# Low bits of weight words kept in PSUM, eight short warm-up series and a new order table in a local-attention and gated-convolution kernel

## The chip, the cores and the metric

One core of a Trainium2 chip runs the whole kernel. TensorE (PE) multiplies matrices and writes its sums to PSUM; VectorE (DVE), ScalarE (ACT) and GpSimd (POOL) do the elementwise work; SyncE (SP) starts the transfers in the order of its queue. The metric is device time per execution in microseconds, the median of the runs.

## The reference

There are 4 batches of 768 positions with 8 heads of 64 (512 columns). The first stage is attention: every query sees the keys less than 16 positions away and, beside them, 24 pooled keys, each the largest entry by column of a block of 32 keys; the pooled values are block means.

```
scores_l = scale * q @ k.T, where |i - j| < 16, else -1e9
scores_s = scale * q @ k_max + log(32)        # k_max: 24 blocks
a = softmax(concat(scores_l, scores_s)); x = a @ concat(v, v_mean)
```

The second stage takes x as (batch, position, 512). A causal convolution of five taps by column gives a gate, and two 512x512 matrices frame it:

```
gate = 1 / (1 + exp(-conv5(x, conv_w)))
out = (gate * (x @ w_val)) @ w_out
```

q and k are drawn at 0.8, conv_w at 24 / sqrt(5), x and the result are float32. The two matrices and conv_w reach the kernel as float64 words.

## The kernel before

A tile of queries has 64 positions; a group g is four of them (256 positions, all 512 columns), and there are 12 groups, three to a batch. A unit u is half a group: two head pairs, so that unit u belongs to group u // 2 and there are 24.

For one unit the work goes through these steps, each named by a letter in the order table: `S` score products on TensorE (two per unit, by head pair), `N` mask and row minimum on VectorE (four), `E` exponentials with row sums on ScalarE (four steps of two activations and two reads of the accumulator), `R` reciprocals, `M` the scaling by them on GpSimd (two), `T` transposes on TensorE, `C` their eviction on ScalarE (two), `X` the product with the values. `F` and `H` copy its result to SBUF (float32 and rounded to the matrix format), `L` is the rest that the rounding lost, `I`, `A` and `G` are the convolution (a first tap, four more taps of two column blocks on VectorE, a tanh), all by unit. For a group there are `V` (product with w_val, two per group), `gf`, `gh`, `gl` (gating, rounding and rest), `O` (product with w_out, two per group), `oe` (eviction of the output) and `st` (its store).

The first batch has a special way to its pooled values: `VB` sums them on TensorE into the two tiles `vb`, and `X` of group 0 multiplies with them apart. For the other groups small copies `f` write the pooled rows into the value tile (four per group, waiting for that tile's loads). Group 0 also does its `V` and `O` in float32, in one series of four terms each, from the tile `wf`; all others use the split weights (high and low part, `wvc`/`wvb`, `woc`/`wob`).

The matrices come as float64 words in four blocks of 128 rows. A block's path is: load (`w.k`, `o.k`), `rescale` on ScalarE (line 387, `wvs`, `wos`: the high word as a float, rebiased), `low_bits` on VectorE (line 395, `wvd`, `wod`: the low word shifted right by 29), `join` on VectorE (line 402, `wve`, `woe`: high part shifted and or-ed with the low bits). `cs`, `cd`, `ce` do the same for the 20 convolution weights. Both matrices go through the one tile `wf`, one behind the other: the second can be written only after group 0's `V` has read the first.

The order of all work is a table written out by hand, `ORDER` (line 53): the program walks over its tokens and issues each, so every engine, and SP's queue too, works through its own share in that order and waits where something isn't ready. `psum_plan` (line 131) gives each PSUM tile one of four single banks (`p`) or two double ones (`s`, for scores and transposes) by the first and the last token that uses it; a tile that takes a bank waits until the one before it has been read. `pw` (line 329) are products of a constant tile with itself, whose result nobody reads: six series of two, all in one bank that they hold from the first to the last of them.

Of the kernel before, what the change touches and what calls it, by code (L numbers as in the profile page):

```python
# [53 lines left out]
k.0.1 mset pw.0 q0.1 ks.0.1 k.0.0 ks.0.0 kc.0.1 S.0.1 pw.1 pw.2 kc.0.0 c cs q0.0 m N.0.3 E.0.3 N.0.2
E.0.2 S.0.0 N.0.1 E.0.1 N.0.0 E.0.0 q.1 S.2.0 N.2.1 S.2.1 k.0.3 ks.0.3 q0.3 n.0.2 VB.2 kc.0.3 pw.3
E.2.1 S.1.1 N.2.0 E.2.0 N.2.2 E.2.2 N.2.3 E.2.3 S.3.1 k.0.2 q0.2 ks.0.2 N.1.3 E.1.3 R.0 kc.0.2 n.0.4
w.0 wvs.0 i h.0 S.1.0 N.1.1 E.1.1 cd ce N.1.2 E.1.2 S.3.0 N.3.1 N.1.0 n.0.0 pw.4 VB.4 wvd.0 E.1.0
w.1 wvs.1 N.3.2 wve.0 N.3.3 VB.0 n.0.5 wvd.1 M.0.1 M.0.0 T.0 C.0.1 C.0.0 R.1 M.1.1 n.0.3 VB.5 VB.3
N.3.0 R.2 E.3.1 E.3.0 q.2 S.5.1 S.5.0 E.3.3 wve.1 E.3.2 N.5.0 M.2.1 N.5.3 N.5.2 N.5.1 S.4.1 wvc.1
S.4.0 n.0.1 VB.1 M.1.0 T.1 vb.0 vb.1 C.1.0 E.5.0 R.3 N.4.3 v.0.1 v.0.0 w.3 wvs.3 X.0 I.0.1 F.0 I.0.0  # L60
N.4.1 wvd.3 N.4.0 N.4.2 wve.3 w.2 wvd.2 C.1.1 M.3.0 wvc.0.1 v.1.1 X.1 v.1.0 A.0.0 A.0.1 A.0.2 M.3.1
A.0.3 k.1.3 wvb.0 M.2.0 T.2 wvs.2 E.5.1 wve.2 I.1.1 F.1 A.0.4 I.1.0 A.1.0 A.0.5 wvb.1 k.1.0 h.1
wvc.2.1 A.1.1 A.0.6 ks.1.3 kc.1.3 T.3 C.3.0 V.0.0 C.2.1 E.5.2 C.2.0 wvc.3.1 A.0.7 k.1.1 ks.1.1
kc.1.1 ks.1.0 wvb.3 kc.1.0 E.5.3 R.5 E.4.3 M.5.1 q.3 S.6.1 E.4.2 n.1.1 E.4.0 A.1.2 M.5.0 pw.5 G.0
N.6.3 gf.0.0 A.1.3 E.4.1 N.6.2 A.1.4 R.4 f.1.0.1 f.1.1.0 f.1.1.1 f.1.0.0 X.2 C.3.1 H.2 k.1.2 M.4.0
X.3 F.2 F.3 I.2.0 H.3 ks.1.2 I.3.0 S.6.0 N.6.0 N.6.1 v.2.1 T.5 C.5.1 C.5.0 A.1.5 v.2.0 A.3.0 A.2.0
I.3.1 S.7.1 A.1.6 A.3.1 A.1.7 A.3.2 kc.1.2 S.7.0 N.7.0 A.3.3 o.1 E.6.0 E.6.2 n.1.0 q.4 N.7.3 A.3.4
N.7.2 A.3.5 M.4.1 T.4 E.6.3 C.4.0 G.1 C.4.1 I.2.1 E.7.3 E.7.0 N.7.1 A.3.6 V.0.1 wod.1 tr.1.1 S.9.0
tr.1.0 gf.0.1 o.0 A.3.7 A.2.1 wod.0 A.2.2 wos.0 wos.1 woe.0 woe.1 G.3 f.2.0.0 f.2.0.1 o.2 E.7.2
S.8.1 wvb.2 L.3 wod.2 S.8.0 S.9.1 f.2.1.0 f.2.1.1 o.3 X.5 wod.3 wos.2 woe.2 h.2 L.2 woc.1.1 wos.3  # L70
woe.3 n.1.3 tr.1.3.1 F.5 E.6.1 H.5 E.7.1 X.4 F.4 H.4 woc.2 O.0.1 oe.0.1 O.0.0 A.2.3 R.6 M.6.0 A.2.4
N.9.0 M.6.1 A.2.5 N.8.3 A.2.6 R.7 A.2.7 I.5.0 G.2 I.5.1 I.4.0 N.8.1 N.8.0 N.9.1 n.1.2 tr.1.2 N.8.2
A.4.0 woc.0 v.3.0 k.2.2 k.2.3 N.9.2 A.4.1 A.5.0 v.4.1 E.8.0 n.2.0 oe.0.0 q.5 A.4.2 A.5.1 v.3.1 E.8.2
V.1.1 N.9.3 VS.1 A.5.2 gf.1.1 E.8.3 I.4.1 vs.1 T.6 L.4 M.7.0 M.7.1 T.7 C.6.1 wob.0 E.9.1 v.4.0 C.7.1
ks.2.3 kc.2.3 A.5.3 k.2.1 A.4.3 C.7.0 L.5 woc.3.1 wob.3 gh.1.1 A.5.4 f.3.1.0 f.3.0.0 f.3.0.1 wob.2
A.5.5 h.3 C.6.0 E.8.1 E.9.2 V.1.0 A.4.4 A.4.5 f.3.1.1 f.4.0.0 S.11.1 S.11.0 A.5.6 ks.2.2 kc.2.2
S.10.0 A.5.7 E.9.0 G.5 A.4.6 S.10.1 gf.1.0 R.8 M.8.0 A.4.7 k.3.2 X.7 wob.1 gl.1.1 M.8.1 X.6 E.9.3
V.2.1 N.10.1 N.11.0 G.4 N.11.2 N.10.3 N.11.3 N.10.0 N.10.2 H.7 F.7 gh.1.0 I.7.0 R.9 I.7.1 q.6 k.2.0
st.0.0 v.5.0 A.7.0 E.10.0 M.9.0 M.9.1 gf.2.1 V.2.0 q.7 f.4.1.1 f.4.0.1 f.4.1.0 T.9 E.10.3 A.7.1
I.6.0 F.6 A.7.2 gl.1.0 E.10.2 H.6 ks.2.1 I.6.1 N.11.1 E.10.1 A.7.3 st.0.1 k.3.0 v.5.1 ks.2.0 kc.2.1  # L80
A.6.0 A.7.4 A.7.5 T.8 A.6.1 C.8.0 R.10 C.9.1 E.11.3 C.9.0 C.8.1 A.6.2 A.7.6 E.11.0 A.6.3 gf.2.0 h.4
L.7 kc.2.0 tr.2.0 O.1.0 oe.1.0 A.6.4 S.13.0 S.12.1 S.12.0 S.13.1 A.7.7 N.13.1 A.6.5 M.10.1 L.6
M.10.0 E.11.1 E.11.2 A.6.6 R.11 M.11.0 M.11.1 G.7 X.8 n.2.1 tr.2.1 f.5.1.0 gh.2.0 gl.2.0 H.8 X.9 F.9
O.1.1 A.6.7 N.12.3 G.6 N.13.0 st.1.0 N.12.1 f.5.0.0 N.13.3 N.12.2 q.8 n.2.2 I.8.1 I.8.0 F.8 I.9.0
oe.1.1 N.13.2 N.12.0 h.5 A.8.0 A.8.1 I.9.1 E.12.3 H.9 L.9 T.10 C.10.1 gh.2.1 T.11 C.11.1 E.12.1
E.12.2 C.10.0 A.9.0 C.11.0 gl.2.1 L.8 A.9.1 A.9.2 A.9.3 A.9.4 V.3.0 A.8.2 tr.2.2 gf.3.0 v.6.0 v.6.1
A.9.5 E.13.2 E.12.0 A.9.6 A.9.7 k.3.3 A.8.3 A.8.4 A.8.5 A.8.6 A.8.7 R.12 M.12.0 O.2.0 G.9 E.13.1
oe.2.0 V.3.1 gf.3.1 E.13.3 E.13.0 M.12.1 gh.3.1 n.2.3 tr.2.3 f.5.0.1 f.5.1.1 X.11 I.11.1 X.10 G.8
gl.3.1 I.11.0 H.11 S.14.1 S.15.0 n.3.1 st.2.0 R.13 S.14.0 F.11 S.15.1 VS.2 vs.2 k.3.1 O.2.1 F.10
I.10.1 H.10 I.10.0 N.15.1 N.14.0 A.11.0 N.15.0 N.15.2 N.14.1 A.11.1 A.11.2 N.15.3 A.11.3 M.13.0  # L90
N.14.3 V.4.0 A.10.0 N.14.2 A.10.1 A.10.2 A.10.3 oe.2.1 E.15.0 L.10 h.6 gf.4.0 M.13.1 n.3.2 tr.3.2
st.1.1 gh.3.0 gl.3.0 T.13 E.14.0 T.12 C.12.1 E.14.1 V.4.1 gh.4.0 gl.4.0 E.14.3 C.13.1 E.14.2 C.12.0
A.11.4 A.10.4 A.11.5 ks.3.1 A.11.6 A.11.7 O.3.0 ks.3.0 kc.3.0 S.17.1 C.13.0 E.15.1 L.11 f.6.0.1
E.15.2 gf.4.1 tr.3.1 S.17.0 G.11 f.6.0.0 v.7.0 f.6.1.1 A.10.5 A.10.6 A.10.7 ks.3.3 R.14 M.14.1
M.14.0 S.16.0 st.2.1 E.15.3 G.10 gh.4.1 v.7.1 S.16.1 N.16.2 N.16.1 n.3.3 oe.3.0 q.9 f.6.1.0 X.13
H.13 F.13 X.12 F.12 I.13.1 I.13.0 kc.3.1 R.15 M.15.0 N.16.0 N.17.3 N.16.3 N.17.0 ks.3.2 N.17.1
N.17.2 E.17.3 E.17.2 V.5.0 I.12.0 H.12 E.17.0 T.14 M.15.1 n.3.0 tr.3.0 gf.5.0 C.14.0 f.7.0.1 A.12.0
f.7.0.0 I.12.1 E.16.0 tr.3.3 gl.4.1 A.13.0 A.13.1 kc.3.3 A.13.2 A.13.3 A.12.1 T.15 A.13.4 A.12.2
A.12.3 E.17.1 R.17 A.12.4 A.13.5 A.13.6 C.14.1 A.12.5 O.3.1 C.15.0 gh.5.0 oe.3.1 E.16.2 V.5.1 gf.5.1
M.17.1 L.12 E.16.3 q.10 O.4.0 v.8.0 f.7.1.0 st.3.1 f.7.1.1 E.16.1 R.16 M.16.1 oe.4.0 C.15.1 v.8.1  # L100
X.14 gl.5.0 kc.3.2 h.7 X.15 A.13.7 G.13 A.12.6 A.12.7 F.15 I.14.0 G.12 S.18.1 S.18.0 S.19.0 st.4.0
f.8.1.1 S.19.1 q.11 gh.5.1 gl.5.1 O.5.0 N.18.1 H.14 F.14 M.17.0 L.14 I.14.1 I.15.1 H.15 L.15 M.16.0
I.15.0 oe.5.0 N.18.3 N.18.0 N.19.1 N.19.0 A.14.0 E.19.0 st.3.0 f.8.1.0 f.8.0.0 f.8.0.1 N.19.3 N.19.2
A.14.1 A.14.2 N.18.2 E.19.2 L.13 O.4.1 oe.4.1 VS.3 h.8 T.16 C.16.1 A.14.3 A.14.4 A.14.5 A.14.6
A.15.0 A.14.7 C.16.0 E.18.3 G.14 v.9.0 v.9.1 vs.3 f.9.0.0 st.5.0 T.17 C.17.0 C.17.1 A.15.1 A.15.2
E.18.2 V.6.1 gf.6.1 A.15.3 A.15.4 A.15.5 A.15.6 V.6.0 gf.6.0 f.9.1.0 E.18.1 E.18.0 R.18 E.19.1
E.19.3 R.19 X.17 F.17 H.17 M.19.1 X.16 I.16.0 v.11.1 f.9.1.1 A.15.7 G.15 H.16 F.16 gh.6.1 I.16.1
S.23.1 gl.6.1 S.20.1 S.20.0 S.23.0 N.23.0 M.19.0 N.20.2 N.20.1 E.20.1 E.20.2 A.16.0 N.20.3 N.23.3
N.23.1 A.16.1 V.7.1 O.5.1 gh.6.0 E.20.3 N.23.2 A.16.2 gf.7.1 N.20.0 I.17.1 I.17.0 oe.5.1 M.18.1
M.18.0 T.18 C.18.1 gh.7.1 gl.6.0 h.9 T.19 C.19.1 st.4.1 O.6.1 V.7.0 A.17.0 A.17.1 A.17.2 st.5.1  # L110
v.11.0 f.9.0.1 C.19.0 C.18.0 A.17.3 A.17.4 A.17.5 A.16.3 f.11.1.0 f.11.0.0 E.23.3 E.23.1 E.20.0
oe.6.1 A.16.4 A.16.5 A.17.6 A.16.6 A.16.7 A.17.7 gf.7.0 X.19 R.20 L.17 M.20.1 X.18 E.23.2 G.16
S.22.0 S.21.0 S.22.1 S.21.1 L.16 V.8.1 G.17 E.23.0 R.23 M.23.0 I.18.1 I.18.0 N.21.1 gh.7.0 H.19
gl.7.0 gl.7.1 F.18 v.10.0 F.19 H.18 L.19 N.21.2 E.21.2 N.21.3 O.7.1 st.6.1 v.10.1 f.11.1.1 N.21.0
E.21.0 f.10.1.1 f.10.0.0 A.18.0 A.18.1 N.22.0 A.18.2 gf.8.1 I.19.0 I.19.1 A.18.3 M.20.0 E.21.1
E.21.3 R.21 oe.7.1 V.8.0 M.21.1 st.7.1 A.19.0 A.19.1 f.10.0.1 A.19.2 A.19.3 N.22.1 A.19.4 O.6.0
M.21.0 T.21 gf.8.0 gh.8.0 M.23.1 N.22.2 E.22.2 E.22.1 L.18 N.22.3 A.19.5 A.18.4 oe.6.0 st.6.0 A.18.5
T.20 C.20.1 O.7.0 A.19.6 A.19.7 E.22.3 E.22.0 R.22 C.21.1 gh.8.1 gl.8.0 V.9.1 C.20.0 A.18.6 G.19
gl.8.1 f.10.1.0 M.22.1 M.22.0 h.10 oe.7.0 st.7.0 gf.9.1 C.21.0 A.18.7 G.18 X.20 f.11.0.1 X.21 F.20
I.20.1 H.20 I.20.0 T.23 A.20.0 T.22 O.8.0 I.21.0 I.21.1 H.21 F.21 C.22.0 A.20.1 A.20.2 A.21.0 A.21.1  # L120
A.21.2 A.21.3 A.21.4 A.20.3 A.21.5 L.21 oe.8.0 st.8.0 gh.9.1 A.20.4 A.20.5 A.20.6 O.8.1 oe.8.1
st.8.1 C.22.1 C.23.0 C.23.1 V.9.0 L.20 V.10.0 h.11 gl.9.1 A.21.6 A.21.7 gf.9.0 gh.9.0 gl.9.0 A.20.7
G.20 X.23 F.23 H.23 L.23 G.21 X.22 I.23.0 gf.10.0 gh.10.0 I.23.1 O.9.1 oe.9.1 O.9.0 H.22 I.22.0 F.22
# [582 lines left out]
```

## Time and profile before

| | before |
|---|---|
| median of 3 runs | 240.81 us (240.70 to 241.55) |
| profiled execution | 242.98 us, span 241.2 us |
| TensorE busy | 221.4 us (92%), 2884 records |
| ScalarE | 186.4 us (77%) |
| VectorE | 171.4 us (71%) |
| GpSimd | 155.8 us (65%) |
| transfers | 46.42 MB, mean 192 GB/s |
| mean granted TensorE clock | 0.991 |

The span runs from the first to the last instruction of the core; the time of an execution is a little longer. The profiled execution is one of its own and took longer than the median of the runs. The busy shares are means over the span, and the stretches of the kernel differ: the rows further down are read by stretch.

### The profile page before, as it was taken

Reading aid. Unit: us, or ns where it says so; the run is one execution under the profiler, and the core shown is the slowest. Engines: PE = TensorE matmul, PEld = TensorE weight load, DVE = VectorE, ACT = ScalarE, POOL = GpSimd, SP = SyncE. Lnnn points to the kernel's source line nnn. Section 1 sums busy time; section 2 is a strip of 40 time slices with the busy share of each in tenths; the row PEclk is TensorE's granted clock in tenths of the full one; section 3 lists DMA queues with packets and bytes.
Section 4 is the critical chain, followed back from the end, with each engine's and each line's share of the span. In section 5 each row is a group of like instructions: output and inputs, shape, how many; then the busy total and the mean of one; then the engine's idle time right before and its main releaser. Section 6 shows DMA issues by size and latency. Waiting matters only on the chain.

```text
span 241.2 us, 7772 instructions
## 1 busy us (share of the span) xinstructions
PE 221.4 (92%) x2884; PEld 187.3 (78%) x2884; DVE 171.4 (71%) x683; ACT 186.4 (77%) x614; POOL 155.8 (65%) x219
## 2 busy tenths in 40 slices
...
DMA packets 17318, 46.42 MB, mean 192 GB/s; under 512 B 2400, under 2 KB 3424, under 8 KB 17280
## 3 DMA queue, kind: packets, MB, share of 16 engines
...
q8 instruction: 23, 0.38, 0.6%
q14 instruction: 15, 0.12, 0.2%
...
## 4 chain that ended last, share of the span: by engine, by line
PE 71%; POOL 9%; DVE 6%; DMA 5%; ACT 4%; issue 3%; SPq 1%; POOLq 0%; ACTq 0%; DVEq 0%
PE val L567 26%; PE out L596 23%; PE x L513 9%; PE s L444 7%; POOL p L487 4%; PE pt L496 4%; DMA v<-vb 2%; DVE sn L460 2%; POOL vT L326 2%; DMA k<-in_kT_dram 1%; DVE wf L409 1%; POOL xl L533 1%; POOL gl L581 1%; DVE g L547 1%; ACT g L542 1%
## 5 line engine op out<-in xcount | busy, mean ns | idle before, releaser
L547 DVE SCALAR_TENSOR_TENSOR g<-xf,cwt,g 128x256 f32<-128x256 f32 x192 | 88.4, 483 | 12.4 <-ACT g L542 8.8
L474 ACT ACTIVATE p<-sn,nm 128x120 f32<-128x120 f32 x192 | 73.9, 397 | 5.9 <-DVE nm L460 3.0
L487 POOL TENSOR_TENSOR p<-p,ri 128x480 f32<-128x480 f32 x48 | 47.3, 1001 | 22.5 <-DVE ri L482 18.3
L460 DVE CUSTOM_DVE_ANT_0 sn<-s,mask 128x120 f32<-128x120 f32 x192 | 42.4, 276 | 14.7 <-PE s L444 14.3
L567 PE MATMUL val<-xh,wv 128*128 128x256 f32 x352 | 50.1, 284 | 0.0
L567 PEld LDWEIGHTS val<-xh,wv 128*128 128x128 f32 x352 | 45.3, 188 | 1.9 <-issue 0.6
L596 PE MATMUL out<-wo,gh 128*128 128x512 f32 x176 | 45.6, 401 | 0.0
L581 POOL TENSOR_TENSOR gl<-gf,gh 128x512 fp32r<-128x512 f32 x22 | 28.4, 1294 | 19.8 <-ACT gh L576 18.7
L474 ACT ACTIVATION_READ_ACCUMULATOR p<-sn,nm 128x1 f32 x192 | 38.5, 201 | 0.0
L596 PEld LDWEIGHTS out<-wo,gh 128*128 128x128 f32 x176 | 31.8, 188 | 7.4 <-ACT g L542 0.4
L533 POOL TENSOR_TENSOR xl<-xf,xh 128x512 fp32r<-128x512 f32 x22 | 28.4, 1295 | 9.2 <-ACT xf L528 6.6
L444 PE MATMUL s<-k,qbd 64*64 64x120 f32 x768 | 25.3, 279 | 6.8 <-POOL k L315 3.5
L444 PEld LDWEIGHTS s<-k,qbd 64*64 64x64 f32 x768 | 21.1, 140 | 11.0 <-POOL k L315 6.3
L326 POOL TENSOR_TENSOR vT<-vT 128x384 f32<-128x384 f32 (+3 forms) x48 | 27.2, 566 | 2.8
L513 PE MATMUL x<-pts,v 120*64 120x64 f32 x768 | 27.2, 224 | 1.9 <-DMA v<-vb 1.2
L513 PEld LDWEIGHTS x<-pts,v 120*64 120x64 f32 x768 | 25.3, 138 | 3.9 <-issue 1.8
L567 PE MATMUL val<-xl,wv 128*128 128x256 f32 x176 | 27.8, 279 | 0.0
L500 ACT COPY pts<-pt 120x512 f32<-120x512 f32 x48 | 26.7, 592 | 1.4 <-PE pt L496 1.3
L572 DVE SCALAR_TENSOR_TENSOR gf<-gt,val 128x512 f32<-128x512 f32 x24 | 16.4, 685 | 13.2 <-PE val L567 12.8
L596 PE MATMUL out<-wo,gl 128*128 128x512 f32 x88 | 24.3, 396 | 0.2 <-POOL gl L581 0.2
L567 PEld LDWEIGHTS val<-xl,wv 128*128 128x128 f32 x176 | 23.8, 188 | 0.0
L606 ACT ACTIVATE ob<-out 128x512 f32<-128x512 f32 x23 | 13.8, 599 | 11.6 <-PE out L596 7.6
...
## 6 DMA issues: line engine op xcount, KB each, us to landing
v<-in_vw_dram SPq DMA_DIRECT2D x24, 512.0 KB
k<-in_kT_dram SPq DMA_DIRECT2D x16, 478.0 KB
out_dram<-ob SPq DMA_DIRECT2D x23, 256.0 KB
qbd<-in_qT_dram SPq DMA_DIRECT2D x11, 512.0 KB
vT<-in_vT_dram SPq DMA_DIRECT2D x12, 384.0 KB
raw_wv<-in_wv_dram SPq DMA_DIRECT2D x4, 512.0 KB
raw_wo<-in_wo_dram SPq DMA_DIRECT2D x4, 512.0 KB
...
```

What stands on the lines that cost most here:

```text
L326: nc.gpsimd.tensor_tensor(dst, src[:, :, :n], src[:, :, n : 2 * n], ALU.add)
L444: nc.tensor.matmul(sp[64 * e : 64 * e + 64, h, c * KW : c * KW + KW], qbd[g % NQB][64 * h : 64 * h + 64, pr, i * QT : i * QT + QT], ktile( ...
L460: nc.vector.tensor_tensor_reduce(sn[:, n, :], tiles["s", u][:, h, c * KW : c * KW + KW], mask[:, mv, :], -1.0 / math.sqrt(D), 3.0e38, ALU.add,
L474: nc.scalar.activation(p[:, n, :], tiles["sn", u][:, n, :], AF.Exp, bias=tiles["nm", u][:, n : n + 1], scale=-1.0, accum_out=rs[:, u % NRS ...
L487: nc.gpsimd.tensor_tensor(p[:, w], p[:, w], ri[:, w].unsqueeze(2).broadcast_to([P, TPU, KW]), ALU.mult)
L500: nc.scalar.copy(pts[:, :, QT * e : QT * e + QT], tiles["pt", u][:KW, e])
L513: nc.tensor.matmul(dst, v[:KW, i, c0 : c0 + D], src, start=True, stop=g > 0)
L533: nc.gpsimd.tensor_tensor(xl[:, prs(u), :], xf(g)[:, prs(u), HALO:], tiles["xh", g][:, prs(u), :].bitcast(F32), ALU.subtract,)
L547: nc.vector.scalar_tensor_tensor(gt, xf(u // NHP)[:, pr, o : o + SG], cwt[:, pr, o : o + 1], gt, ALU.mult, ALU.add)
L567: nc.tensor.matmul(val[:, r], w, x, start=(n == 0), stop=(n == len(terms) - 1))
L581: nc.gpsimd.tensor_tensor(gl[:, cos, :], tiles["gf", g, cp], tiles["gh", g][:, cos, :].bitcast(F32), ALU.subtract)
L596: nc.tensor.matmul(po, x, w, start=(n == 0), stop=(n == len(terms) - 1))
```

## The change

The shift `low_bits` writes its result to a PSUM tile of its own, and `join` reads it from there and no longer from the target tile. `psum_plan` learns these nine tiles, each of which holds a single bank from shift to join. Every `pw` series gets a bank of its own for as long as it lasts, and there are eight series, one of eight products and seven of two. The order table is replaced as a whole; all other tokens are the same ones as before. The first 17 and the last 5 lines of the new table are shown.

```diff
-NWARM = 2
+NWARM = (8, 2, 2, 2, 2, 2, 2, 2)
...
+mset k.0.0 pw.2 k.0.1 h.0 ks.0.1 kc.0.1 pw.6 pw.0 pw.3 q0.1 S.0.1 q0.0 c k.0.2 ks.0.0 kc.0.0 m S.0.0
+N.0.1 ks.0.2 kc.0.2 cs E.0.1 N.0.0 n.0.2 E.0.0 pw.5 pw.4 VB.2 N.0.2 E.0.2 k.0.3 N.0.3 ks.0.3 q0.2
+S.1.0 N.1.0 N.1.1 E.0.3 E.1.0 q.1 S.3.0 kc.0.3 S.3.1 N.3.0 q0.3 S.1.1 N.1.3 N.1.2 pw.1 N.3.3 N.3.2
+R.0 M.0.0 M.0.1 pw.7 N.3.1 w.1 wvs.1 wvd.1 E.1.1 E.1.2 E.1.3 R.1 M.1.1 w.0 wvs.0 n.0.0 VB.0 wve.1
+E.3.0 n.0.1 S.2.0 S.2.1 N.2.2 N.2.0 cd N.2.3 wvd.0 n.0.5 VB.1 wve.0 N.2.1 n.0.4 i w.2 wvd.2 M.1.0
+E.3.1 wvs.2 E.3.2 ce E.3.3 R.3 T.0 C.0.0 E.2.1 C.0.1 wve.2 wvc.0.1 M.3.1 M.3.0 q.2 n.0.3 VB.4 VB.5
+VB.3 vb.0 w.3 wvd.3 wvs.3 v.0.0 vb.1 S.5.1 S.5.0 N.5.0 wvc.2.1 wve.3 N.5.2 T.1 C.1.0 E.2.2 C.1.1
+N.5.3 N.5.1 v.0.1 X.0 F.0 wvb.2 I.0.0 E.5.1 X.1 I.1.0 F.1 I.1.1 k.1.3 ks.1.3 wvb.0 E.2.3 k.1.2 A.0.0
+ks.1.2 A.0.1 A.0.2 A.1.0 A.1.1 wvc.3.1 A.0.3 A.1.2 S.4.1 T.3 E.2.0 R.2 n.1.1 tr.1.1 kc.1.3 A.1.3
+S.4.0 N.4.0 wvc.1 V.0.1 kc.1.2 I.0.1 A.0.4 A.1.4 A.0.5 A.1.5 E.5.2 A.0.6 v.1.1 v.1.0 E.5.3 k.1.1 o.2
+n.1.3 A.1.6 C.3.1 f.1.0.0 q.3 C.3.0 N.4.2 E.5.0 N.4.3 R.5 N.4.1 h.1 M.2.1 A.1.7 M.2.0 A.0.7 f.1.0.1
+V.0.0 ks.1.1 T.2 E.4.0 wos.2 wvb.1 G.1 G.0 E.4.3 wod.2 gf.0.0 n.1.2 E.4.1 C.2.1 M.5.1 wvb.3 o.0
+wod.0 woe.2 S.7.1 S.7.0 f.1.1.0 f.1.1.1 X.3 k.1.0 ks.1.0 C.2.0 wos.0 X.2 woe.0 o.1 wod.1 gf.0.1 H.3
+F.3 wos.1 woe.1 tr.1.2 kc.1.1 S.6.1 kc.1.0 S.6.0 N.6.1 woc.0 o.3 E.4.2 wos.3 wod.3 woe.3 O.0.0 H.2
+F.2 O.0.1 I.2.1 I.2.0 tr.1.3.1 M.5.0 woc.1.1 N.6.2 N.7.2 I.3.0 E.6.1 I.3.1 N.6.3 A.2.0 A.2.1 N.6.0
+E.6.0 E.6.3 A.2.2 N.7.0 A.2.3 v.3.1 N.7.3 N.7.1 q.4 L.3 n.1.0 v.2.0 v.2.1 tr.1.0 L.2 woc.3.1 A.2.4
+A.2.5 R.4 M.4.0 E.6.2 oe.0.0 oe.0.1 k.2.2 T.5 C.5.0 S.8.1 S.8.0 f.2.0.0 M.4.1 R.6 M.6.1 E.7.2 C.5.1
...
+gf.10.0 gl.9.0 G.21 X.22 I.22.0 H.22 gh.10.0 F.22 L.22 gf.10.1 gh.10.1 X.23 gl.10.0 I.22.1 H.23
+gl.10.1 O.9.0 O.10.1 F.23 oe.9.0 A.22.0 A.22.1 A.22.2 A.22.3 A.22.4 A.22.5 I.23.1 A.22.6 I.23.0
+A.23.0 A.22.7 G.22 A.23.1 A.23.2 A.23.3 A.23.4 A.23.5 L.23 V.11.0 A.23.6 gf.11.0 V.11.1 O.10.0
+oe.10.1 st.10.1 gh.11.0 A.23.7 G.23 oe.10.0 gf.11.1 gh.11.1 gl.11.1 O.9.1 st.9.0 oe.9.1 st.9.1
+st.10.0 gl.11.0 O.11.0 oe.11.0 st.11.0 O.11.1 oe.11.1 st.11.1
...
@@ -147,9 +147,13 @@
             return [("val", a[0], a[1])]
         if name in ("O", "oe"):
             return [("out", a[0], a[1])]
+        if name in ("cd", "ce"):
+            return [("low", "cw", 0)]
+        if name in ("wvd", "wve", "wod", "woe"):
+            return [("low", name[:2], a[0])]
         if name == "VB":
             return [("vb", 0), ("vb", 1)]
-        return {"vb": [("vb", a[0])], "VS": [("vsp", a[0])], "vs": [("vsp", a[0])], "pw": [("pw", 0)]}.get(
+        return {"vb": [("vb", a[0])], "VS": [("vsp", a[0])], "vs": [("vsp", a[0])], "pw": [("pw", a[0])]}.get(
             name, []
         )
 
@@ -328,9 +332,9 @@
 
     def op_pw(k):
         t = tiles["ones"]
-        for j in range(NWARM):
+        for j in range(NWARM[k]):
             nc.tensor.matmul(
-                ps(("pw", 0), [P, DM])[:QT, : QT + BASE], t[:, :QT], t[:, : QT + BASE],
+                ps(("pw", k), [P, DM])[:QT, : QT + BASE], t[:, :QT], t[:, : QT + BASE],
                 start=True, stop=True,
             )
 
@@ -397,17 +401,18 @@
             return
         dst, raw, n, bufs = parts(nm, k)
         low = raw.rearrange("p (n two) -> p two n", two=2)[:, 0]
-        nc.vector.tensor_scalar(dst.bitcast(U32), low, 29, None, ALU.logical_shift_right)
+        t = ps(("low", nm, k), [P, n])
+        nc.vector.tensor_scalar(t.bitcast(U32), low, 29, None, ALU.logical_shift_right)
 
     def join(nm, k):
         if not wide:
             if nm != "cw":
                 nc.vector.tensor_copy(wf[:, k], rawt(nm, k).bitcast(F32))
             return
-        d = parts(nm, k)[0].bitcast(U32)
-        sc = tiles["sc", f"{nm}{k}"]
+        sc, low = tiles["sc", f"{nm}{k}"], tiles["low", nm, k]
         nc.vector.scalar_tensor_tensor(
-            d, sc.bitcast(U32), 3, d, ALU.logical_shift_left, ALU.bitwise_or
+            parts(nm, k)[0].bitcast(U32), sc.bitcast(U32), 3, low.bitcast(U32),
+            ALU.logical_shift_left, ALU.bitwise_or,
         )
 
     def high_part(nm, k, alt=0):
```

## Rows read from the trace of the kernel before

**Rows 1.** Stretches: us, PE, PEld, DVE, ACT, POOL busy, granted clock, DMA share, GB/s.

```profile
0.00:26.43 26.43, 19.40 (x269) 12.20 (x269) 17.17 (x105) 17.60 (x73) 8.26 (x25) 1.00 0.88 314
26.43:57.58 31.15, 24.78 (x489) 21.01 (x485) 26.37 (x90) 26.65 (x90) 23.76 (x37) 0.95 0.97 348
47.05:53.80 6.75, 5.87 (x32) 4.57 (x32) 4.05 (x23) 5.99 (x22) 4.87 (x7) 0.75 0.94 312
57.58:64.70 7.12, 7.12 (x22) 3.29 (x19) 6.94 (x39) 7.12 (x21) 6.81 (x9) 1.00 0.46 151
64.70:237.20 172.50, 170.10 (x2117) 150.80 (x2115) 120.91 (x455) 134.46 (x432) 117.00 (x151) 1.00 0.46 149
237.20:241.20 4.00, 0.00 (x0) 0.00 (x0) 0.00 (x0) 0.60 (x1) 0.00 (x0) 0.88 0.27 106
```

**Rows 2.** TensorE's timeline: start us, us, line, operation, count, idle before and releaser.

```profile
1.51 0.95 PE L332 MATMUL pw<-ones 128*64 128x104 f32 x4 [1.51 <-POOL ones L255]
5.92 1.08 PE L444 MATMUL s<-k,qbd 64*64 64x120 f32 x16 [3.46 <-POOL k L315]
26.43 0.34 PE L513 MATMUL x<-pts,v 120*64 120x64 f32 x4
31.66 1.15 PE L496 MATMUL pt<-ident,p 64*120 64x64 f32 x32
33.19 3.72 PE L567 MATMUL val<-xf,wf 128*128 128x256 f32 x16 [0.38 <-ACT g L542]
53.76 1.87 PE L444 MATMUL s<-k,qbd 64*64 64x120 f32 x64
55.56 2.08 PE L513 MATMUL x<-pts,v 120*64 120x64 f32 x64
57.58 7.13 PE L596 MATMUL out<-wf,gf 128*128 128x512 f32 x16
```

**Rows 3.** Transfers by line: count, KB of each.

```profile
v<-in_vw_dram SPq DMA_DIRECT2D x24, 512.0 KB
k<-in_kT_dram SPq DMA_DIRECT2D x16, 478.0 KB
qbd<-in_qT_dram SPq DMA_DIRECT2D x11, 512.0 KB
vT<-in_vT_dram SPq DMA_DIRECT2D x12, 384.0 KB
raw_wo<-in_wo_dram SPq DMA_DIRECT2D x4, 512.0 KB
vn<-in_vn_dram SPq DMA_DIRECT2D x6, 256.0 KB
```

**Rows 4.** ScalarE's timeline, its first exponential and four steps later on.

```profile
8.14 0.40 ACT L474 ACTIVATE p<-sn,nm 128x120 f32<-128x120 f32 x1 [0.93 <-DVE nm L460]
...
22.01 0.40 ACT L474 ACTIVATE p<-sn,nm 128x120 f32<-128x120 f32 x1
...
25.05 0.62 ACT L417 CAST wv<-wf 128x512 fp32r<-128x512 f32 x1
```

**Rows 5.** Tiles of VectorE: count, ns least/median/most, first and last start.

```profile
L400 DVE TENSOR_SCALAR wf<-raw_wv x4: 415/474/1414, 19.8 to 29.3; 128x512 uint32<-128x512 uint32 x4
L409 DVE SCALAR_TENSOR_TENSOR wf<-sc_wv,wf x4: 679/780/1083, 20.6 to 32.6; 128x512 uint32<-128x512 uint32 x4
...
L572 DVE SCALAR_TENSOR_TENSOR gf<-gt,val x24: 676/686/689, 39.6 to 227.0; 128x512 f32<-128x512 f32 x24
```

**Rows 6.** GpSimd's timeline around the slowest shift.

```profile
28.73 1.72 POOL L421 TENSOR_TENSOR wv<-wf,wv 128x512 fp32r<-128x512 f32 x1
```

**Rows 7.** Waits of SP's queue: in total, times, longest.

```profile
SPq L373 <- DMA v<-in_vw_dram: 28.5, 9, 5.1
```

**Rows 8.** ScalarE's timeline at the end.

```profile
234.42 0.39 ACT L603 ACTIVATE ob<-out 128x256 f32<-128x256 f32 x1 [2.20 <-PE out L596]
237.68 0.60 ACT L606 ACTIVATE ob<-out 128x512 f32<-128x512 f32 x1 [2.87 <-DMA out_dram<-ob]
```

More of the change, by code (lines that the diff above doesn't have):

```diff
@@ L50 @@
 NRS = 4
-NWARM = 2
+NWARM = (8, 2, 2, 2, 2, 2, 2, 2)
 ORDER = """
[L54 to L123, printed above, removed]
```

56 lines of the change are left out of this document (52 added, 4 removed).

## Prediction

> **What bounds the kernel now.** I read four views: the busy time of every engine by stretch, TensorE's timeline, the lists of transfers and queue waits, and the other engines' rows where TensorE waits.
>
> The stretches show three regimes [rows 1]. From 64.70 to 237.20 us TensorE is busy 170.10 of 172.50 us while the transfers are at 0.46: there only the amount of products counts, and 2.4 us are all that an order can win. From 237.20 to 241.20 TensorE has nothing: the last output is evicted and stored. All else happens ahead of 57.58, where TensorE is busy 19.40 of 26.43 us and then 24.78 of 31.15 us, 13.4 us idle in all. In the second of these stretches the transfers are at 0.97 and ScalarE works 26.65 us of 31.15: loads and ScalarE set the pace, and TensorE waits. There is a second loss: over 47.05 to 53.80 the granted clock is 0.75 on average, so 3.4 us ran at the lower level of 1.2 GHz, about 1.7 us lost, behind a stretch in which TensorE had kept stopping.
>
> One event closes the start: the first group's two output products `O.0.0` and `O.0.1` (57.58, 7.13 us [rows 2]). They need all four blocks of the second weight matrix, converted. From there on TensorE hardly stops. So I ask when that event comes, and how much product work has by then been left for later.
>
> **The new order, step by step.** Between `X.0` and the output products the old table lets TensorE do `X.0 X.1 T.2 T.3 V.0 S.6 pw.5 X.2 X.3 T.5 S.7 T.4 S.9 S.8 X.5 X.4`; the new one has `X.0 X.1 S.4 T.3 V.0 T.2 S.7 X.3 X.2 S.6`. (`S.4` was ahead of `X.0`.) Left for later are T.4 and T.5 (1.08 by the pitch of a 1.15 us row of two), S.8 and S.9 (1.80), X.4 and X.5 (2.05), together 4.93 us [rows 2]. If `O.0` starts at time t, the end moves by t + 4.93 - 57.58: no change at t = 52.65.
>
> When can it start?
> - Loads. Up to the last block of the second matrix the old table issues 16,504 KB and the new one 15,160 KB, counted over the tables with the sizes of [rows 3] (first matrix as the second, the first q in four of 128). The new amount is 15.52 MB. By 26.43 us 314 GB/s have moved 8.30 MB; the other 7.22 MB at 348 GB/s take 20.7 us [rows 1]: landed at 47.2. Rescaling and joining add 0.68 each, giving 48.6. Only the last quarter of `O.0.0` reads that block, 2.7 us behind its start, so loads allow t = 45.9.
> - ScalarE. Up to the last rescaling the old table gives it 30 exponential steps and 41 others, the new one 24 and 31. A step of four instructions takes 0.76 us (four steps from 22.01 to 25.05 [rows 4]), the others about 0.52 (an estimate: rows of 0.60 and 0.62 [rows 4, 8], of which some 0.1 overlaps the next): 44.1 us before, 34.4 after. It starts later: 8.14 before [rows 4]; the new table puts the K block whose scores come first second in the queue (478 KB at 314 GB/s, 1.6 us) and lets the first exponential wait for the second score product: I take 10.2. Done at 44.6, with 1 to 3 us of idle time at 46 to 48; the last join is then done about when the loads have it.
> - TensorE. `X.0` needs the first values, 8,320 KB into the queue: 27.1 against 26.43. Then X.0 and X.1 with their extra half (4.2), S.4, S.6, S.7 (2.7), T.2 and T.3 (1.08), V.0 (twice 3.7) and X.2 with X.3 (2.05) are 17.4 us, so it is free at 44.5 and then waits.
>
> How far does a real start lie behind such sums? The old table's loads land at 51.1 and its ScalarE is through at 8.14 + 44.1 + 1 = 53.2; `O.0` began at 57.58, 4.4 us behind the later of the two. For the new table the later one is 47.2, or 45.6 for ScalarE with the same 1 us. I let a little over half of the slip return, as TensorE stands idle ahead of `O.0` and may fall to the lower clock, and take t = 50.0: 50.0 + 4.93 - 57.58 = -2.65.
>
> The end: the old table's last eviction, of 512 columns on one engine, waits until 237.68 for a store that stands behind another in SP's queue, 0.5 us after TensorE; its split one took 0.39 [rows 8]. The new table ends with the split one, and no store that it needs stands behind it: 0.5 + 0.2 less, -0.7. Between the two I leave the 2.4 us of idle time as they are; bounds 0 and 5, twice what they are.
>
> **Low bits in PSUM.** Nine shifts and nine joins stay; their operand moves. A shift between two SBUF tiles takes 0.415 at best, and 1.414 once, over a GpSimd subtraction that itself took 1.72; no row has a shift that writes PSUM, so between 0.415 and the 0.686 of a 512-column operation that reads PSUM [rows 5, 6]. A join took 0.679 to 1.083 and should stay at 0.68. Eight large shifts at +0.27 are +2.2 us of VectorE at worst; with the worst overlaps gone (1.0 on the shift, 0.4 and 0.2 on joins) -1.6 at best. VectorE is busy 26.37 of 31.15 us there [rows 1], so part of either would count; I take 0, as both are small beside the half slip. The shifts of the second matrix no longer write the tile that `V.0` reads, so they leave the wait for `V.0`; but the new table ends `V.0` some 5 us before that matrix is complete, so that is worth nothing by itself. New waits: `X.2` takes a bank that a stored block holds until its join, with T.5 and the S products queued behind it on TensorE; that block is the 11.95th MB, landed at 36.9, ahead of `X.2` at 42.6.
>
> Of that overlap the rows show that the shift lost 1.0 us and that both ran at once [rows 5, 6]. The Trainium skill (SBUF — State Buffer, "SBUF: two separate sides") says why: such VectorE operations and GpSimd take one pair of ports by turns, each for a whole instruction. Against the change speaks the Trainium skill's page VectorE: DVE Perf Modes ("Why PSUM operands drop a tier"): VectorE's doubled rate for float32 is for SBUF alone, and no row here shows a shift without it. By the first rule the sum is about -1.6 us of VectorE, by the second +2.2; both lie inside the bounds above.
>
> **Extra products.** 22 instead of 12; two took 0.95 at the start (a product shows as two records [rows 2]). Fourteen now stand ahead of the first score product: 6.7 us at that pace, until 8.2, where the K block allows 7.5. At most 0.7 us late, and faster if the clock rises meanwhile (16 score records took 1.08 at 5.92, where 64 took 1.87 later). Nothing of it reaches `X.0`, which waits for loads until 27.1: 0, bounds 0 and +0.7. The one product series in the thin stretch around 39 is gone, so the lower clock can return there: 0 to +1.7, inside the slip.
>
> **Sum.** -2.65 - 0.7 = -3.35. The profiled execution took 242.98 (241.2 span, 1.8 around it) and becomes 239.6; the median of the runs, 2.2 lower, goes from 240.81 to 237.5.
>
> **Rivals.**
> - The full gain: no slip, t = 47.2: -5.45 - 0.7, 234.7. For it: loads and ScalarE meet there. Against: no start in this trace met its bound. Chance 0.10.
> - The wait only changes its name: the slip of 4.4 returns (t = 51.6), or 1 to 2 us of new idle time later. GpSimd's share, M.2 and the pooled keys of S.6, is as likely a culprit as the banks. -1.05 - 0.7, and 0.9 as half of a clock that falls again: 240.0. Chance 0.22, half of it within 0.5%.
> - Slower: the weights stand behind held copies. In the new table three of the four blocks stand in SP's queue behind the first of the four small copies `f.1`, and such copies held that queue for 28.5 us in nine waits, up to 5.1 [rows 7]. Behind the load that the first copy awaits, 1,374 KB (`k.1.1`, `o.2`, `n.1.3`) are still under way, 4.0 us at 348 GB/s, so a hold must exceed that. Two holds of 5.1 less 4.0 are 6.2 us: t = 50 + 6.2 = 56.2, which is +3.5 - 0.7, and 1.7 more if TensorE, blocked at `O.0`, falls to 1.2 GHz: 243.6 to 245.3. It decides from t = 53.4 on. Against it: what those copies read (vb) is ready early in both tables. Chance 0.12.
> - The change doesn't do what it says for VectorE (PSUM costs what the overlaps gave) is no case of its own: it moves t by at most 1.
>
> **How the numbers follow.** The forecast has 0.56. A measurement tells 0.5%, 1.2 us, from no change: faster means under 239.6. Forecast 0.53, full gain 0.10 and 0.05 of the second rival make 0.68; the same 0.20; slower 0.12. The range goes from 234.8, just above the full gain's point, to 241.0, which holds the renamed wait with all of the 1.7; some 2 in 10 lie outside, most of it above.
>
> **What would show it.** `O.0` starting at 48 to 52, TensorE idle 2 to 5 us just ahead of it, less than 2.5 us idle behind it, and 3.3 us from its last product to the end. Joins all near 0.68, shifts between 0.42 and 0.69, none over 1. Wrong, if `O.0` starts after 52.7, or if idle time behind it exceeds 5 us.

## The result, and the profile after

The changed kernel took 237.38 us (median of 4 runs, 236.75 to 237.97) against 240.96 us (240.70 to 241.55) before: ratio 0.9848, 95% interval 0.9815 to 0.9880, or -3.6 us. In two later comparisons the same kernel gave 0.9852 (0.9812 to 0.9892) and 0.9859 (0.9815 to 0.9903). The forecast was 237.5. The profiled execution took 237.97 us (span 236.2), 0.6 above its median, where that of before was 2.0 above its own; so the two profiles differ by 5.0 us, 1.4 more than the medians, and each step below is weighed against 5.0.

The stretches after, in the columns of [rows 1]; they end and begin where the first group's output products `O.0` begin and end, and at TensorE's last product (26.43 and 64.70 are bounds of [rows 1]; two short stretches are left out).

```profile
0.00:26.43 26.43, 20.61 (x283) 13.71 (x285) 16.94 (x91) 16.45 (x64) 10.16 (x28) 1.00 0.95 359
26.43:46.00 19.57, 17.07 (x320) 14.62 (x316) 17.39 (x57) 17.65 (x62) 15.58 (x29) 1.00 0.93 339
47.25:56.01 8.76, 8.76 (x20) 3.53 (x16) 8.35 (x46) 6.28 (x24) 8.08 (x13) 0.81 0.69 243
64.70:232.23 167.53, 167.52 (x2114) 147.48 (x2112) 119.54 (x466) 136.44 (x434) 110.83 (x142) 1.00 0.48 155
232.23:236.20 3.97, 0.00 (x0) 0.00 (x0) 0.42 (x1) 0.38 (x1) 0.00 (x0) 0.91 0.21 68
```

The first line moved 359 GB/s where before moved 314. The fourth has no idle time on TensorE (167.52 of 167.53); before had 2.4 us of it. The third is `O.0` with a clock of 0.81. The last, from the last product to the end, is 3.97; before it was 4.06, from the end of the last product at 237.14.

TensorE's timeline around `O.0` says where it starts and what it waits for just ahead.

```profile
32.09 7.17 PE L572 MATMUL val<-xf,wf 128*128 128x256 f32 x32
...
46.68 0.64 PE L449 MATMUL s<-k,qbd 64*64 64x120 f32 x16 [1.79 <-POOL vT L330]
47.25 8.83 PE L601 MATMUL out<-wf,gf 128*128 128x512 f32 x16
```

`O.0` starts 10.3 us earlier than in [rows 2], but takes 8.83 us instead of 7.13. Both halves of `V.0` are over at 39.3; before, the second began at 48.42:

```profile
47.93 0.56 PE L496 MATMUL pt<-ident,p 64*120 64x64 f32 x12 [1.74 <-issue]
48.42 5.41 PE L567 MATMUL val<-xf,wf 128*128 128x256 f32 x16
```

It came behind a stop of 1.74 us and took 5.41 us, where both halves together take 7.17 after. From there to `O.0` TensorE had no idle time ([rows 2], 53.76 to 57.58), so in this profile `O.0` came late because `V.0` did, and did not itself wait for the conversions. They waited for `V.0` as well. The conversions of the second matrix on VectorE show it: first before, then after.

```profile
53.01 0.43 DVE L400 TENSOR_SCALAR wf<-raw_wo 128x512 uint32<-128x512 uint32 x1 [2.33 <-PE val L567]
...
56.06 1.28 DVE L409 SCALAR_TENSOR_TENSOR wf<-sc_wo,wf 128x512 uint32<-128x512 uint32 x2
57.26 0.75 DVE L400 TENSOR_SCALAR wf<-raw_wo 128x512 uint32<-128x512 uint32 x2
57.93 1.28 DVE L409 SCALAR_TENSOR_TENSOR wf<-sc_wo,wf 128x512 uint32<-128x512 uint32 x2
```

```profile
40.04 0.69 DVE L405 TENSOR_SCALAR low_wo<-raw_wo 128x512 uint32<-128x512 uint32 x1
...
41.74 0.69 DVE L405 TENSOR_SCALAR low_wo<-raw_wo 128x512 uint32<-128x512 uint32 x1 [0.43 <-DMA raw_wo<-in_wo_dram]
...
48.62 0.69 DVE L413 SCALAR_TENSOR_TENSOR wf<-sc_wo,low_wo 128x512 uint32<-128x512 uint32 x1
```

Before, the first shift stood 2.33 us waiting for `V.0` (the line in brackets), and all four blocks were converted behind it, 53.0 to 59.2. ScalarE, whose rescaling each join needs too, stood behind VectorE there and ended its last rescaling at 58.07:

```profile
55.06 0.60 ACT L553 ACTIVATE gt<-g 128x512 f32<-128x512 f32 x1 [1.95 <-DVE g L547]
...
56.78 1.29 ACT L393 ACTIVATE sc_wo<-raw_wo 128x512 f32<-128x512 f32 x2 [0.36 <-DVE wf L409]
```

After, the blocks are converted one by one from 40.0 on, and one shift waits 0.43 us for its load instead. The tiles answer to [rows 5] (ns least/median/most):

```profile
L405 DVE TENSOR_SCALAR low_wv<-raw_wv x4: 687/690/692, 16.1 to 23.6; 128x512 uint32<-128x512 uint32 x4
L413 DVE SCALAR_TENSOR_TENSOR wf<-sc_wv,low_wv x4: 636/661/687, 17.0 to 25.5; 128x512 uint32<-128x512 uint32 x4
```

And the end of the run answers to [rows 8]: the two halves of the last eviction, by ScalarE and VectorE, go one behind the other.

```profile
232.26 0.38 ACT L608 ACTIVATE ob<-out 128x256 f32<-128x256 f32 x1 [2.15 <-PE out L601]
232.67 0.42 DVE L609 TENSOR_SCALAR ob<-out 128x256 f32<-128x256 f32 x1 [7.80 <-ACT ob L608]
```

### The profile page after: what moved, and what is told of

Read it like the earlier page. It is cut to its first block, busy times and chain, and to the rows that moved or that the text cites. A ratio compares the mean times of both kernels' runs of the same rounds, so it can differ in the third digit from the quotient of the medians.

```text
span 236.2 us, 7826 instructions
## 1 busy us (share of the span) xinstructions
PE 223.2 (95%) x2904; PEld 187.8 (80%) x2904; DVE 170.1 (72%) x683; ACT 186.9 (79%) x614; POOL 152.7 (65%) x219
## 4 chain that ended last, share of the span: by engine, by line
PE 80%; DMA 12%; SPq 2%; DVE 2%; ACT 2%; POOL 1%; issue 1%; DVEq 0%
PE out L601 31%; PE val L572 27%; PE x L518 10%; PE s L449 7%; PE pt L501 5%; DMA k<-in_kT_dram 5%; DMA v<-in_vw_dram 3%; DMA vn<-in_vn_dram 3%; DVE g L552 1%; PE x L520 1%; POOL vT L330 1%; PE vsp L364 1%; SPq L275 1%; SPq L377 0%; DVE ks L306 0%
## 5 line engine op out<-in xcount | busy, mean ns | idle before, releaser
L552 DVE SCALAR_TENSOR_TENSOR g<-xf,cwt,g 128x256 f32<-128x256 f32 x192 | 87.2, 485 | 14.6 <-ACT g L547 8.5
L492 POOL TENSOR_TENSOR p<-p,ri 128x480 f32<-128x480 f32 x48 | 46.6, 989 | 23.9 <-DVE ri L487 10.9
L572 PE MATMUL val<-xh,wv 128*128 128x256 f32 x352 | 49.5, 283 | 0.0
L572 PEld LDWEIGHTS val<-xh,wv 128*128 128x128 f32 x352 | 44.5, 188 | 1.1 <-issue 0.3
L479 ACT ACTIVATION_READ_ACCUMULATOR p<-sn,nm 128x1 f32 x192 | 37.8, 197 | 0.0
L518 PE MATMUL x<-pts,v 120*64 120x64 f32 x768 | 27.9, 224 | 1.7 <-DVE gf L577 0.5
L449 PEld LDWEIGHTS s<-k,qbd 64*64 64x64 f32 x768 | 19.8, 133 | 8.8 <-POOL k L319 2.2
L547 ACT ACTIVATE g<-x,cwt 128x256 f32<-128x256 f32 x40 | 18.2, 457 | 6.7 <-PE x L518 3.5
```

What stands on the lines that cost most here:

```text
L449: nc.tensor.matmul(sp[64 * e : 64 * e + 64, h, c * KW : c * KW + KW], qbd[g % NQB][64 * h : 64 * h + 64, pr, i * QT : i * QT + QT], ktile( ...
L479: nc.scalar.activation(p[:, n, :], tiles["sn", u][:, n, :], AF.Exp, bias=tiles["nm", u][:, n : n + 1], scale=-1.0, accum_out=rs[:, u % NRS ...
L492: nc.gpsimd.tensor_tensor(p[:, w], p[:, w], ri[:, w].unsqueeze(2).broadcast_to([P, TPU, KW]), ALU.mult)
L518: nc.tensor.matmul(dst, v[:KW, i, c0 : c0 + D], src, start=True, stop=g > 0)
L552: nc.vector.scalar_tensor_tensor(gt, xf(u // NHP)[:, pr, o : o + SG], cwt[:, pr, o : o + 1], gt, ALU.mult, ALU.add)
L572: nc.tensor.matmul(val[:, r], w, x, start=(n == 0), stop=(n == len(terms) - 1))
```

## The experiments

Theory: the order table alone makes the gain, by bringing `O.0` forward. Rivals: the PSUM tiles do, or the extra products (through the clock). Each round ran beside the kernel before on the same chip; ratios are to it. The first four ran together (before: 241.13 us).

**New order, low bits in SBUF.** The nine low-bit tiles of the bank plan go as well.

```diff
-        t = ps(("low", nm, k), [P, n])
-        nc.vector.tensor_scalar(t.bitcast(U32), low, 29, None, ALU.logical_shift_right)
+        nc.vector.tensor_scalar(dst.bitcast(U32), low, 29, None, ALU.logical_shift_right)
```

> The new order and its eight series, with the low bits in the target tile again. If the gain is the order's alone, it stays at 237.4 (within 0.6) and O.0 starts at 47 to 48. If the PSUM tiles give a share, because VectorE's shifts and joins no longer run beside GpSimd, it is 238.4 or more, shifts or joins of over 1 us come back, and O.0 starts at least 1 us later. If PSUM costs something, it is 236.8 or less.

Measured 236.41 us, ratio 0.9835 (0.9755 to 0.9914): the whole gain without PSUM. Two of VectorE's tile rows, then `O.0` in TensorE's timeline:

```profile
L400 DVE TENSOR_SCALAR wf<-raw_wv x4: 637/998/1209, 17.3 to 24.5; 128x512 uint32<-128x512 uint32 x4
L409 DVE SCALAR_TENSOR_TENSOR wf<-sc_wo,wf x4: 697/904/1302, 42.5 to 48.4; 128x512 uint32<-128x512 uint32 x4
```

```profile
46.59 7.22 PE L596 MATMUL out<-wf,gf 128*128 128x512 f32 x16
```

The operations do get slower in SBUF, joins up to 1.30 us against 0.64 to 0.69 in PSUM, but `O.0` starts no later: the new order leaves that much room. The Trainium skill (SBUF — State Buffer, "SBUF: two separate sides") says that a VectorE operation with two SBUF inputs and a GpSimd operation that reads SBUF lock each other out for a whole instruction; the joins' 0.64 to 0.69 with one input in PSUM and up to 1.30 with both in SBUF agree.

**Old order, low bits in PSUM.** The other half alone: old table, `NWARM = (2, 2, 2, 2, 2, 2)`, the rest as changed.

> The old order with the low bits in PSUM and each of the six series in a bank of its own. If the order is all, 240.9 (within 0.6). If the PSUM tiles give a share of their own, 239.9 or less, with all joins near 0.68 us.

Measured 244.26 us (240.19 to 245.13, 4 runs, three of them above 244; no ratio was taken). TensorE's timeline in one of the three:

```profile
56.82 3.84 PE L518 MATMUL x<-pts,v 120*64 120x64 f32 x64 [2.89 <-DVE wf L413]
60.59 5.85 PE L601 MATMUL out<-wf,gf 128*128 128x512 f32 x13
```

The product `X` waits 2.89 us for the bank that a block's low bits hold until its join, and `O.0` starts 3 us later than before. That is the new wait which the prediction named for `X.2`; in this execution of the old order it is real. No run of this kernel shows a gain (the shortest, 240.19, lies within the runs of the kernel before); what the tiles cost here is not shown.

**New order, no extra products.** `NWARM` all zero.

> The new order with none of the 22 extra products. By the prediction they are worth nothing, since X.0 waits for loads until about 26 us in any case: 237.4 (within 0.6), with the clock up only after 12 us. If the early clock carries into the sum through earlier scores and exponentials, it is 238.2 or more and X.0 starts at least 1 us later.

Measured 236.35 us, ratio 0.9860 (0.9757 to 0.9963). TensorE's timeline, its first products and `O.0`:

```profile
6.80 1.95 PE L449 MATMUL s<-k,qbd 64*64 64x120 f32 x32 [6.80 <-POOL k L319]
...
45.06 7.61 PE L601 MATMUL out<-wf,gf 128*128 128x512 f32 x16
```

Without them the first score products run at half the pace (1.95 us for 32 records, where later ones take 1.05), yet nothing later is later. They are worth nothing here. So the gain stays without the tiles and without the extra products; a run of the new order without both was not made.

**Old order, 14 products first.** The kernel before with `NWARM = (14, 2, 2, 2, 2, 2)` in place of 2.

> The old order and low bits in SBUF, with 14 extra products ahead of the first score product. By the prediction 0, at most 0.7 slower: 240.9 to 241.6. If an early clock is worth something of itself, 240.2 or less.

Measured 238.78 us (ten runs, one of them apart at 427.12), ratio 0.9944 (0.9893 to 0.9995), some 1.3 us of the 3.6, where 0 or slower was expected. TensorE's timeline, then VectorE's:

```profile
43.69 3.72 PE L567 MATMUL val<-xf,wf 128*128 128x256 f32 x16
...
52.15 1.98 PE L596 MATMUL out<-wf,gf 128*128 128x512 f32 x4
55.92 5.55 PE L596 MATMUL out<-wf,gf 128*128 128x512 f32 x12 [1.78 <-DVE wf L409]
```

```profile
52.20 2.26 DVE L400 TENSOR_SCALAR wf<-raw_wo 128x512 uint32<-128x512 uint32 x2
54.38 2.48 DVE L409 SCALAR_TENSOR_TENSOR wf<-sc_wo,wf 128x512 uint32<-128x512 uint32 x2
```

`V.0` and `O.0` come some 5 us earlier, and now `O.0` stops for a join: behind `V.0`, the conversions are the old order's next bound. Two shifts take 2.26 us where before they took 0.75, and the two joins behind them 2.48 where they took 1.28: 2.7 us more, in operations that ran beside GpSimd's. So the tiles, worth nothing in the new order, might be worth something in the old one once `V.0` comes early; that was not tried. How the products bring `V.0` forward is not shown by a run of its own; up to 26.43 us this kernel moved 349 GB/s where before moved 314.

The next four ran together (before: 240.65 us). Open was what sets `O.0` in the new order. **The changed kernel again:**

> The changed kernel itself, unaltered, as a measure beside the other three. If the lower clock at O.0 in its profile (47.8 to 51.2 us, some 1.7 us lost) is a chance of the one execution, this profile shows O.0 in 7.1 to 7.3 us and a profiled time near 236.3; if it belongs to the order, O.0 takes 8.5 to 8.9 us again and the profiled time is 237 to 238.

Measured 236.55 us. This profile has `O.0` from 46.74 in 7.13 us, without the fall of the clock, ahead of it a wait of 1.54 us, and a span of 235.0.

Theory: the loads; rival: ScalarE and the scores. **Loads of the second matrix later.** In the table `v.2.0 v.2.1` move from behind `L.3 n.1.0` to just ahead of `o.1`.

> The changed kernel with the two loads v.2.0 and v.2.1 (1 MB, which group 2 needs) put ahead of the second, third and fourth last-needed blocks o.1 and o.3. Theory loads: O.0 ends when the last block has come, so the start of O.0 or a wait inside it moves its end by about 1 MB at 345 GB/s, 2.9 to 3.1 us, and the kernel by 2.5 to 3.2 us (ratio to the changed kernel about 1.012). Rival, ScalarE and the chain of scores set O.0 at 47.25: nothing, under 0.5 us.

Measured 239.44 us, 2.9 more than the unaltered kernel; ratio 0.9950 (0.9910 to 0.9989). `O.0` in TensorE's timeline:

```profile
46.42 1.12 PE L601 MATMUL out<-wf,gf 128*128 128x512 f32 x2
50.41 8.83 PE L601 MATMUL out<-wf,gf 128*128 128x512 f32 x14 [2.87 <-DVE wf L413]
```

Much the same start, and then 2.87 us of waiting for a join whose load came late: about the time of one MB. So the loads bound `O.0` in the new order, with little to spare; its start hangs on the scores just ahead of it (46.68, behind 1.79 us). The 2.9 us of the medians are not this wait alone: in this profile the clock fell too (its 14 records took 8.83 us, where they take 6.39 in the third profile of the unaltered kernel) and `O.0` ended at 59.17, 5.4 us later than in the profile above, and two of the twelve runs took 236.69 and 237.94.

**Last output product in two banks.** `O.11.1` as two series of 256 columns; VectorE evicts the second.

```diff
+        for c in range(halves):
+            po = ps(("outb", g, si) if c else ("out", g, si), [P, DM])
+            cs = slice(c * DM // halves, (c + 1) * DM // halves)
             for n, (x, w) in enumerate(terms):
-                nc.tensor.matmul(po, x, w, start=(n == 0), stop=(n == len(terms) - 1))
+                nc.tensor.matmul(po[:, cs], x, w[:, cs], start=(n == 0), stop=(n == len(terms) - 1))
```

> The changed kernel with the last output product O.11.1 as two series of 256 columns in two banks, so that VectorE's half of the eviction need not wait for ScalarE's half of the same bank. Theory bank: the halves were evicted one behind the other because they share a bank (0.38 then 0.42 us); now the first half goes while TensorE computes the second, and the time from the last product to the end falls from 3.97 to 3.4 to 3.6 us, so 0.4 to 0.6 us less in all (less what narrower products cost). Rival, the store alone sets the end: 3.9 to 4.0 as before, no gain.

Measured 236.00 us, ratio 0.9818 (0.9773 to 0.9863), 0.55 under the unaltered one. The timeline of the end:

```profile
232.14 0.38 ACT L613 ACTIVATE ob<-out 128x256 f32<-128x256 f32 x1 [0.79 <-PE out L605]
232.79 0.55 PEld L605 LDWEIGHTS outb<-wo,gl 128*128 128x128 f32 x4
232.90 0.64 PE L605 MATMUL outb<-wo,gl 128*128 128x256 f32 x4
233.64 0.43 DVE L614 TENSOR_SCALAR ob<-outb 128x256 f32<-128x256 f32 x1 [7.52 <-PE outb L605]
```

VectorE now waits for TensorE and no longer for ScalarE. From the last product (233.54) to the end (236.7) are 3.2 us instead of 4.0, and the product itself takes 3.03 instead of 2.96.

**Products ahead of `O.0` to hold the clock.** `pw.8`, six products of the identity with itself, between `S.6.1` and `S.6.0`.

> The changed kernel with six products of a constant tile with itself between S.6.1 and S.6.0, where TensorE stood idle for 1.79 us ahead of O.0. Theory clock: the idle time ahead of O.0 is what lowered the clock behind it, so with the filler O.0 takes 7.1 to 7.3 us instead of 8.8 and the kernel gains 1.2 to 1.7 us against an execution that has the dip. Rival: the dip comes from earlier stops (41 to 44 us) or is a chance of the execution, then within 0.5 us of the changed kernel, with or without a dip.

Measured 237.18 us (236.13 to 239.53), ratio 0.9885 (0.9819 to 0.9951): 0.6 over the unaltered one, with runs that overlap it. TensorE's timeline ahead of `O.0`:

```profile
47.23 1.28 PE L336 MATMUL pw<-ident 128*64 128x104 f32 x12 [1.28 <-DVE gf L577]
48.44 0.64 PE L449 MATMUL s<-k,qbd 64*64 64x120 f32 x16
49.01 7.13 PE L601 MATMUL out<-wf,gf 128*128 128x512 f32 x16
```

The clock stays up, but the filler waits 1.28 us (by the releaser for a bank of its own, held until `gf` has read it), and `O.0` starts 2.3 us behind that of the unaltered kernel: more than the fall costs. Not all of it is the filler's: the scores ahead of it, `S.6.1`, already start at 45.31 where they started at 43.99.

The last four ran together (before: 240.61 us). **Old order, loads ahead of the held `q.2`:** `n.0.1 v.0.1 v.0.0` move to just ahead of `q.2`, which had waited 4.2 us at the head of SP's queue.

> The kernel before with three loads of its table (n.0.1, v.0.1, v.0.0, 1.15 MB) put ahead of the load q.2, which held SP's queue for 4.2 us until a score product had read its buffer. Theory loads: the transfers, which moved 268 GB/s over 17 to 22 us, stay near 400 there, 0.7 to 1.0 MB more by 26.43 us; everything behind comes 2 to 2.9 us earlier, O.0 starts at 54.7 to 55.6 instead of 57.58 and the kernel gains 1.5 to 2.9 us (ratio 0.988 to 0.994). Rival, in the old order ScalarE (through at 53.2 by my sum) or TensorE's waits set O.0: the transfers gain the same, O.0 moves by less than 1 us and the time by less than 0.7 us.

Measured 241.13 us, ratio 1.0049 (1.0020 to 1.0079): 0.5% slower. The stretch from 17 to 22 us, before and with the move, and then its TensorE:

```profile
17.00:22.00 5.00, 4.47 (x50) 2.29 (x44) 4.92 (x30) 4.36 (x16) 1.64 (x2) 1.00 0.80 268
```

```profile
17.00:22.00 5.00, 4.26 (x62) 2.69 (x64) 4.45 (x28) 4.36 (x19) 1.93 (x2) 1.00 1.05 406
```

```profile
46.47 3.72 PE L567 MATMUL val<-xf,wf 128*128 128x256 f32 x16
...
55.67 1.98 PE L596 MATMUL out<-wf,gf 128*128 128x512 f32 x4
58.66 3.83 PE L596 MATMUL out<-wf,gf 128*128 128x512 f32 x8 [1.00 <-DVE wf L409]
```

The transfers got their 400 GB/s, and it brought nothing: my loads theory falls for the old order. The move is not of the loads alone, though: with `q.2` later, `X.0` starts at 27.88 instead of 26.43. Here too `O.0` stops for a join, 8.5 us behind the end of `V.0` (50.2), as it did with 14 products first (47.4 to 55.9); in between stand ScalarE's rescalings (51.7 to 55.9) and again slow shifts and joins (2.25 and 2.48 us for the last two of each).

**The changed kernel a third time:**

> The changed kernel once more, unaltered, beside the next two: 236.0 to 237.4.

Measured 236.77 us; `O.0` waits 0.29 us for a join, no fall of the clock.

**`tr.1.3.1` behind `M.5.0` on GpSimd.**

> The changed kernel with the pooled maxima tr.1.3.1 put behind the scaling M.5.0 on GpSimd. S.6.0 waited until 46.17 and 46.68 in two profiles, 1.8 us behind the end of the copy kc.1.0 that it needs and inside tr.1.3.1. Theory GpSimd: the release comes late because of what follows on GpSimd; with one operation of 1 us there, S.6.0 starts within 1.1 us of the end of kc.1.0 and O.0 at 45.5 to 46.5; O.0's last quarter then waits for the join of the last block (49.4 and 48.9), so it ends 0 to 0.7 us earlier and the kernel gains at most 0.7. Rival, a load releases S.6.0: it starts 1.8 us behind kc.1.0 as before and nothing changes.

Measured 237.03 us, ratio 0.9873 (0.9828 to 0.9919); nothing gained. `S.6.0` in TensorE's timeline:

```profile
46.12 0.64 PE L449 MATMUL s<-k,qbd 64*64 64x120 f32 x16 [1.32 <-POOL p L492]
```

`S.6.0` still starts 1.4 us behind the copy `kc.1.0` (44.71), with other work following on GpSimd. Without extra products `S.6.1` and `S.6.0` ran from 44.08 to 45.06 with no idle time, so that `S.6.0` stood at most 0.4 us behind its copy (44.22; the middle of the row is an estimate), although GpSimd did the same work there as in the changed kernel: what GpSimd does next, which the brackets name, isn't the cause. What is stays open.

**Both:**

> The swap on GpSimd and the last output product in two banks together. If the two gains add, 0.4 to 0.8 us from the end and 0 to 0.7 from the start: 235.4 to 236.0, under both kernels. If a lower clock at O.0 falls in the profile, up to 1.7 more.

Measured 236.26 us, ratio 0.9829 (0.9778 to 0.9880), 0.5 under the unaltered kernel, though its profile has the fall of the clock (`O.0` 8.82 us). The split of the last output gave the same 0.5 twice, with profiles that show how; the runs overlap, and no interval against the changed kernel was taken.

## Why the prediction was right, step by step

The total came out almost to the point, and that is in good part luck: the largest term was 2.75 us off, and errors of the other sign, with the height of the two profiled executions, made up for it. What was right is the mechanism (the new order brings `O.0` forward, and the loads bound it; neither the tiles nor the extra products matter there).

- **The start of `O.0`.** Predicted at 50.0, with a little over half of the slip of 4.4 returning; it came at 47.25, at 46.74 and 45.89 in the repeats. None of the slip returned, 2.75 us better than the step says: this is the start of the rival with the full gain (47.2, chance 0.10), ahead of the 48 to 52 that were to show the forecast, and TensorE stood idle 1.3 to 1.8 us ahead of it, not 2 to 5. The slip was no general lag. It hung on the late second half of `V.0` (48.42, behind a stop of 1.74 us and 1.7 us longer than the 3.72 of the first): `O.0` followed it without a stop, and VectorE's first shift waited 2.33 us for it, ScalarE 1.95 us for VectorE, so that ScalarE was through at 58.07 where the sum has 53.2. In both experiments that brought `V.0` forward in the old order, `O.0` stopped for joins. I had noted that the new table ends `V.0` early and called that worth nothing; by these rows it is what removed the slip. No run moved `V.0` alone, so that is argued and not shown.
- **Loads as the next bound.** Right in kind: with a megabyte more ahead of the matrix `O.0` waited 2.87 us. The rate was too low (359 instead of 314 GB/s up to 26.43, 1.19 MB); I took over a rate in which SP's queue had stood still behind `q.2`, and with that load moved the old order has 351.
- **The clock.** Named as part of the slip; in the profiled execution it fell inside `O.0`, which took 8.76 us up to the next product where before it took 7.13: +1.6. Two of three profiles of the changed kernel don't have it.
- **Idle time behind `O.0`.** Left at 2.4; it is 0, -2.4 (about 0.5 in the repeats).
- **Product time.** 56.01 to 232.23 is 176.2 us, where the old rows without their idle time and with the 4.93 us left for later give 57.58 + 7.13 to 237.20, 172.5, less 2.4, plus 4.93: 175.0. The sum is 1.2 us short. Between `O.0` and the last product, TensorE is busy with score products for 13.10 us (448 records) before and 16.12 us (512) after: the 64 more take 3.0 us where 1.80 were allowed. The 1.80 is the pitch of a row of 64; a row of 16 by itself has 0.57 (46.68 to 47.25), so that shorter series are the price is an estimate, and no run tested it.
- **The tail.** -0.7 predicted, -0.1 measured (3.97 where 3.3 was to show it). The split eviction has its second half queued behind the first on one bank; two banks gave 0.8 us in the profile.
- **Low bits in PSUM and extra products.** Both are worth 0 in the new order as predicted, each shown by a run without it. The shift costs 0.69, the upper bound, and the joins are steady at 0.64 to 0.69. That early products can't reach `O.0` does not hold for the old order, where 14 of them gave 1.3 us.

The profiled difference: -5.4 for `O.0` (47.25 + 4.93 - 57.58), +1.6, -2.4, +1.2, -0.1 are -5.1 against -5.0; it closes because the product time is what the other rows leave. The forecast of -3.35 met the medians' -3.6 with two steps too pessimistic (2.75 and 2.4) against 1.6, 1.2 and 0.6 too optimistic, and 1.4 that lies in how far each profiled execution stood above its median. The full gain came at `O.0` and was partly given back behind it. The weights standing behind held copies didn't happen: no join held `O.0` in the three profiles of the changed kernel by more than 0.3 us.
